# New order, buffer and engine tables for a fused RWKV attention and MLP-mixer kernel

## The chip, the cores and the metric

The kernel runs on one core of a Trainium2 chip. The metric is the time of one execution on the device in microseconds; a run's number is the median of its executions. A profiled execution also has a span, from its first to its last instruction, which is a little shorter than its time.

## The reference

Two stages, float32 in and out. First a linear attention with decay, for batch 4, 8 heads, 768 steps and head size 48:

```python
for t in range(S):
    kt, vt, rt = (k[:, :, t], v[:, :, t], r[:, :, t])
    cur = np.einsum('bhd,bhe->bhde', u[None] * kt, vt)
    y[:, :, t] = np.einsum('bhd,bhde->bhe', rt, state + cur)
    state = w[None, :, :, None] * state + np.einsum('bhd,bhe->bhde', kt, vt)
```

Its output, as x of shape (4, 768, 384), goes through a token mixer and a channel mixer:

```python
h = np.maximum(xt @ w_tok1, 0.0) @ w_tok2      # xt: x with steps and channels turned; d_tok 256
u = x + h.transpose(0, 2, 1)
h2 = np.maximum(u @ w_ch1, 0.0) @ w_ch2        # d_ch 1536
return u + h2
```

## The kernel before, in words

Each batch's 768 steps are six chunks of 128 ("b1 c4" is batch 1, chunk 4). Within a chunk the recurrence is a masked product: k and r are scaled by powers of the decay (tiles `kr`), turned so that the head dimension lies on the partitions (`trk` and `tr_ps` on PE and then `rka` and `rkb` for batches 0 and 1; by a DMA transpose into `rk` for batches 2 and 3), multiplied into scores (`at_ps`), masked on DVE (`AT`), and multiplied with v (`vb`) into `y_ps`. The state goes from chunk to chunk through `kv_ps` and `S`. The term with u is a row sum `adg` times v (`yd` or `ydb`); in batches 2 and 3 the row sum comes from two POOL products, `ku` and `rku`, and a reduction on DVE. The sum is the chunk's part of `x_b`.

When a batch's six chunks are there, the mixer follows: hidden (`h_ps` from `x_b` and `wtok`), relu into `h1r`, back (`hT_ps` or `hx_ps`), the sum u (`u_sb`) and its turned form `uT` (by PE for batch 0 and half of batch 1, by a DMA transpose otherwise). The channel MLP of a batch is two halves of 384 steps: 12 steps `up` a half, each three matmuls into `z_ps` (the "z triple"), a relu into `zr`, and then `down`, in which each of three 128-step tiles takes 12 matmuls in three groups of four into `h_ps`; then `osb` and the store.

Nothing of this runs in the order of the code. The function `add` records each operation as a task with a number (in the order of recording), and `Plan.run` emits the tasks in the order of the table `ORDER`. Each engine works through its own part of that order and never passes one task by another, so an instruction that waits holds all behind it on its engine; DMAs issued by SP are held in the same way in SP's queue, and the weight loads in POOL's. Four tables were written by a planner outside the kernel:

- `ORDER`, the order of all tasks.
- `BUFS`, which buffer of each pool each allocation takes. A new tile in a buffer waits for the readers of the old one. Pool `m` has seven PSUM banks, shared by all results of PE but the state.
- `ENGINES`, for each task recorded by `flex` (relus, copies, casts, products) which of its two engines runs it.
- `W_DEP` and `GATES`: for each of the seven weight loads a load of k, r or v that it waits for, and for some loads a weight load that they wait for. Keys are (batch, chunk, which of k, r, v).

The weight loads are, in order: wtok1, wtok2, the first part of wch1 (columns of the first four up steps), its second part (the other eight), and three parts of wch2. `NWARM` warm-up matmuls on a tile of zeros are tasks of PE, and `FILL` names tasks ahead of which PE gets one more. The engine wrapper records every instruction at one place, so all carry line 281 in the profile, and groups are told apart by their tiles.

In batches 2 and 3 the scaled products run on POOL alone (`POOL_ONLY`).

Of the kernel before, what the change touches and what calls it, by code (L numbers as in the profile page):

```python
# [67 lines left out]
    0, 1, 2, 0, 1, 0, 2, 1, 0, 2, 1, 0, 2, 1, 0, 1, 2, 0, 1, 2, 0, 1, 2, 0,  # L68
],
    'AT1': [  # L70
    0, 1, 2, 0, 1, 0, 2, 1, 0, 2, 1, 0, 2, 0, 1, 2, 0, 1, 2, 0, 1, 2, 0, 1,
# [11 lines left out]
    0, 1, 2, 3, 4, 1, 0, 2, 3, 4, 1, 0, 2, 3, 1, 4, 0, 2, 3, 4, 1, 0, 2, 3,  # L83
# [6 lines left out]
    0, 1, 2, 3, 4, 5, 0, 1, 4, 2, 3, 0, 4, 5, 1, 2, 3, 0, 5, 4, 1, 2, 3, 0, 5, 2, 1, 0, 3, 4,  # L90
# [3 lines left out]
    0, 1, 2, 3, 4, 5, 0, 1, 2, 3, 4, 5, 0, 1, 2, 3, 4, 5, 0, 1, 2, 3, 5, 4,  # L94
],
    'ku': [
    0, 1, 2, 0, 0, 0, 2, 0, 1, 2, 1, 2,
# [13 lines left out]
],  # L111
    'osb': [
    0, 1, 2, 0, 1, 2, 2, 2, 1, 0, 0, 1, 2, 0, 1, 2, 0, 1, 2, 0, 1, 2, 0, 1, 2,
],
    'pr': [
    0, 1, 1, 0, 1, 0, 1, 0, 1, 0, 1, 1,
# [3 lines left out]
    0, 1, 2, 3, 0, 1, 3, 2, 0, 1, 2, 3,  # L120
# [9 lines left out]
    0, 1, 0, 1, 0, 1, 0, 1, 0, 1, 0, 1,  # L130
],
    'rt': [
    0, 1, 2, 3, 4, 0, 1, 2, 4, 0, 3, 1,
# [3 lines left out]
    0, 1, 2, 3, 1, 0, 3, 2,  # L137
# [3 lines left out]
],  # L141
    'vb': [
    0, 1, 2, 3, 4, 0, 1, 3, 2, 4, 0, 1, 2, 3, 0, 3, 4, 1, 3, 1, 2, 0, 4, 3,
],
    'vb2': [],
    'vt': [
    0, 1, 2, 3, 4, 5, 0, 1, 3, 2, 4, 5, 0, 1, 3, 2, 4, 5, 0, 1, 3, 2, 4, 5,
],
    'win': [
    0, 1, 2, 1, 0, 2,  # L150
],
    'yd': [
    0, 1, 2, 0, 1, 2, 0, 1, 2, 0, 1, 0, 2, 1, 0, 1, 2, 0,
],
    'ydb': [
    0, 1, 0, 1, 0, 1,
],
    'zr': [
    0, 1, 2, 1, 0, 1, 2, 0,
],  # L160
}
ENGINES = [
# [12 lines left out]
NWARM = 12  # L175
WIDE_AT = [
    0, 1, 2, 3, 4, 5, 6, 7, 8, 9, 10, 11,
]
FILL = {159: 1}
POOL_ONLY = [  # L180
    2, 3,
]
# [1027 lines left out]
```

## Time and profile before

| | |
|---|---|
| median of 3 runs | 164.02 us (163.69 to 164.03) |
| profiled execution | 163.92 us, span 162.2 us, mean granted clock 0.989 |
| PE busy | 153.4 us, 95% of the span |
| DVE, ACT, POOL busy | 112.1, 68.7, 88.8 us |
| DMA | 26.89 MB, 166 GB/s; 87794 of 93061 packets under 512 B |
| chain that ended last | PE 75%, DMA 11%, POOL 5%, DVE 4% |

The chain of waits is followed back from the last instruction; a share of 75% for PE says that for most of the span the next thing to happen was PE's next matmul. Busy times are sums over the span: matmuls overlap each other in the record, so PE's busy time is not its work at full rate. POOL's products take about 1.0 us each (1000 ns for `kr`, 999 for `ku`), the same product on DVE 0.55.

### The profile page before, as it was taken

Reading aid. Unit: us, or ns where it says so; the run is one execution under the profiler, and the core shown is the slowest. Engines: PE = TensorE matmul, PEld = TensorE weight load, DVE = VectorE, ACT = ScalarE, POOL = GpSimd, SP = SyncE. Lnnn points to the kernel's source line nnn. Section 1 sums busy time; section 2 is a strip of 40 time slices with the busy share of each in tenths; the row PEclk is TensorE's granted clock in tenths of the full one; section 3 lists DMA queues with packets and bytes.
Section 4 is the critical chain, followed back from the end, with each engine's and each line's share of the span. In section 5 each row is a group of like instructions: output and inputs, shape, how many; then the busy total and the mean of one; then the engine's idle time right before and its main releaser. Section 6 shows DMA issues by size and latency. Waiting matters only on the chain.

```text
span 162.2 us, 3788 instructions
## 1 busy us (share of the span) xinstructions
PE 153.4 (95%) x1458; PEld 102.5 (63%) x1459; DVE 112.1 (69%) x237; ACT 68.7 (42%) x150; POOL 88.8 (55%) x112
## 2 busy tenths in 40 slices
PE   6887989599999999999999999999999999999992
PEld 1355667367777667676667766676576666666662
DVE  6599994675697569297969928887998257523432
ACT  3988974437942354255434431144214101355000
POOL 7149891009088899799992987999922000000000
PEclk9996899999999999999999999999999999999999
DMA  5999999999999969999999899998792055300222
GB/s 130 221 206 186 161 246 236 208 178 205 200 180 204 174 137 180 230 211 141 240 213 211 177 192 163 220 207 213 121 251 103 0 124 191 73 6 0 96 98 97
DMA packets 93061, 26.89 MB, mean 166 GB/s; under 512 B 87794, under 2 KB 92148, under 8 KB 93044
## 3 DMA queue, kind: packets, MB, share of 16 engines
q1 hardware_dynamic: 90688, 23.40, 73.7%
q0 software_dynamic: 2160, 3.15, 11.5%
q8 instruction: 11, 0.18, 0.5%
q10 hardware_dynamic: 196, 0.11, 0.2%
q14 instruction: 6, 0.05, 0.1%
HBM read 20.46 MB, written 4.72 MB: 155 GB/s over the span
## 4 chain that ended last, share of the span: by engine, by line
PE 75%; DMA 11%; POOL 5%; DVE 4%; issue 2%; ACT 1%; SPq 1%; POOLq 0%; DVEq 0%
PE h_ps L281 33%; PE z_ps L281 24%; DMA wch<-in_moe_w_ch_dram 5%; PE y_ps L281 4%; PE at_ps L281 3%; DMA win<-in_r_dram 3%; PE hT_ps L281 3%; PE kv_ps L281 2%; DMA kt<-in_k_dram 2%; PE trk L281 2%; POOL kr L281 2%; POOL ydb L281 2%; DVE kr L281 1%; PE hx_ps L281 1%; SPq L281 1%
## 5 line engine op out<-in xcount | busy, mean ns | idle before, releaser
L281 PE MATMUL z_ps<-uT,wch 128*128 128x384 bf16 x288 | 52.5, 327 | 1.8 <-DMA wch<-in_moe_w_ch_dram 1.7
L281 PE MATMUL h_ps<-wch,zr 128*128 128x384 bf16 (+1 forms) x300 | 53.9, 319 | 0.0
L281 ACT ACTIVATE zr<-z_ps 128x384 bf16<-128x384 f32 x56 | 27.1, 491 | 41.0 <-PE z_ps L281 40.7
L281 PEld LDWEIGHTS <-wch 128*128 128x128 bf16 x288 | 31.1, 114 | 14.6 <-DMA wch<-in_moe_w_ch_dram 2.2
L281 PEld LDWEIGHTS <-zr 128*128 128x128 bf16 x300 | 27.6, 98 | 15.4 <-issue 0.2
L281 DVE TENSOR_TENSOR AT<-at_ps,mask 128x512 bf16<-128x512 f32 x48 | 30.9, 684 | 3.0 <-PE at_ps L281 3.0
L281 DVE TENSOR_SCALAR zr<-z_ps 128x384 bf16<-128x384 f32 x40 | 21.3, 554 | 11.9 <-PE z_ps L281 9.2
L281 POOL TENSOR_TENSOR yd<-vb,adg 128x384 f32<-128x384 bf16 x18 | 14.8, 829 | 13.0 <-DVE adg L281 5.2
L281 POOL TENSOR_TENSOR kr<-kt,wnat 128x384 bf16<-128x384 f32 x19 | 19.3, 1018 | 2.7 <-DMA kt<-in_k_dram 2.5
L281 ACT CAST vb<-vt 128x384 bf16<-128x384 f32 x22 | 11.1, 513 | 11.5 <-DMA vt<-in_v_dram 9.7
L281 PEld LDWEIGHTS <-kr 128*128 128x128 bf16 x176 | 11.4, 100 | 6.6 <-POOL kr L281 2.0
L281 DVE TENSOR_TENSOR osb<-u_sb,h_ps 128x384 f32<-128x384 bf16 (+1 forms) x16 | 8.4, 528 | 9.9 <-PE h_ps L281 9.4
L281 POOL TENSOR_TENSOR ku<-kt,u_bc 128x384 f32<-128x384 f32 x12 | 12.1, 1009 | 0.8 <-DMA kt<-in_k_dram 0.8
L281 POOL TENSOR_TENSOR rku<-ku,rt 128x384 f32<-128x384 f32 x12 | 11.9, 1004 | 0.4 <-DMA rt<-in_r_dram 0.3
L281 POOL TENSOR_TENSOR kr<-rt,wp 128x384 bf16<-128x384 f32 x12 | 12.0, 1000 | 0.0
L281 PEld LDWEIGHTS <-wtok 128*128 128x128 bf16 x78 | 7.4, 98 | 4.5
L281 DVE TENSOR_TENSOR x_b<-y_ps,yd 128x384 bf16<-128x384 f32 x18 | 9.6, 552 | 0.5 <-PE y_ps L281 0.5
L281 PE MATMUL y_ps<-vb,AT 128*128 128x48 bf16 x192 | 9.0, 184 | 0.0
L281 POOL TENSOR_TENSOR pr<-rka,rkb 128x512 bf16<-128x512 bf16 x2 | 2.3, 1152 | 11.9 <-DVE rka L281 11.9
L281 PE MATMUL h_ps<-x_b,wtok 128*128 128x384 bf16 x48 | 8.8, 326 | 0.0
L281 ACT CAST S<-kv_ps 48x192 bf16<-48x192 f32 x18 | 5.6, 311 | 6.4 <-PE kv_ps L281 3.3
L281 DVE TENSOR_TENSOR u_sb<-x_b,hT_ps 128x384 bf16<-128x384 bf16 x15 | 7.6, 548 | 0.6 <-PE hT_ps L281 0.6
(92 smaller groups left out, 183.1 us busy)
## 6 DMA issues: line engine op xcount, KB each, us to landing
kt<-in_k_dram SPq DMA_DIRECT2D x24, 192.0 KB, 5.1
vt<-in_v_dram SPq DMA_DIRECT2D x24, 192.0 KB, 4.7
out_dram<-osb SPq DMA_DIRECT2D x23, 192.0 KB, 1.9
win<-in_r_dram SPq DMA_DIRECT2D x6, 384.0 KB, 5.1
rt<-in_r_dram SPq DMA_DIRECT2D x12, 192.0 KB, 3.4
wch<-in_moe_w_ch_dram POOLq DMA_DIRECT2D x4, 384.0 KB, 6.8
wtok<-in_moe_w_tok_dram POOLq DMA_DIRECT2D x2, 384.0 KB, 5.9
wch<-in_moe_w_ch_dram POOLq DMA_DIRECT2D x1, 768.0 KB, 12.2
```

The lines of the kernel that those rows point to most:

```text
L281: return lambda *args, **kw: tc.keep_in_program_order(f(*args, **kw))
```

## The change

`ORDER`, `BUFS` and `ENGINES` are replaced as a whole; `W_DEP` and `GATES` are new; two warm-up matmuls and the one fill are gone; an unused empty list is added. No function and no task but those three matmuls changes. 105 tasks change their engine. The planner that wrote the new tables priced a load at 1.07 times its length if the load ahead of it is of the same tensor and 0.92 times otherwise, and judged an order by its mean over six courses of the execution.

```diff
 ORDER = [
-    0, 3, 22, 54, 18, 6, 16, 8, 895, 42, 59, 21, 896, 43, 39, 23, 53, 7, 13, 24, 19, 9, 2, 14, 56, 1, 11,
...
+    0, 3, 13, 54, 18, 6, 8, 895, 1, 19, 56, 2, 14, 896, 4, 42, 15, 17, 5, 59, 9, 7, 24, 43, 11, 22, 39, 53,
...
 ]
 BUFS = {
     'AT0': [
-    0, 1, 2, 0, 1, 0, 2, 1, 0, 2, 1, 0, 2, 1, 0, 1, 2, 0, 1, 2, 0, 1, 2, 0,
+    0, 1, 2, 1, 0, 2, 1, 0, 2, 1, 0, 2, 1, 0, 2, 1, 0, 2, 1, 2, 0, 1, 2, 0,
...
 ENGINES = [
-    0, 0, 1, 0, 1, 1, 1, 1, 1, 0, 1, 0, 1, 1, 1, 0, 0, 0, 1, 0, 1, 1, 1, 1, 0, 1, 1, 0, 0, 0, 1, 1, 0, 0, 0,
...
+    0, 1, 1, 0, 0, 1, 1, 1, 1, 1, 1, 0, 0, 1, 1, 0, 0, 0, 1, 0, 0, 1, 1, 0, 0, 1, 1, 0, 0, 0, 0, 1, 1, 0, 0,
...
 ]
-W_DEP = [(0, 2, 2), (0, 5, 0), (0, 5, 0), (0, 3, 2), (1, 2, 2), (1, 1, 2), (1, 5, 0)]
-GATES = {(2, 0, 2): 1, (2, 4, 1): 3, (3, 1, 0): 2, (3, 1, 1): 6, (3, 5, 2): 5}
-NWARM = 12
+W_DEP = [(0, 2, 2), (0, 4, 2), (0, 3, 0), (0, 1, 2), (1, 2, 2), (1, 3, 0), (1, 2, 0)]
+GATES = {(2, 0, 1): 4, (2, 3, 1): 2}
+NWARM = 10
 WIDE_AT = [
-    0, 1, 2, 3, 4, 5, 6, 7, 8, 9, 10, 11,
+    0, 1, 2, 3, 4, 5, 6, 7, 8, 9,
 ]
-FILL = {159: 1}
+FILL = {}
+TOKQ = []
```

What moves, where the prediction speaks of it (orders of the two programs, engine by engine):

| | before | after |
|---|---|---|
| SP, loads of batch 0 (rw: r window of two chunks) | rw0, rw2, k0, k1, rw4, v1, k3, k2, k4, v0, v2, v3, v4, k5, v5 | rw0, k1, rw2, k0, rw4, k2, k4, v0, v1, k3, v4, v2, k5, v3, v5 |
| POOL, from wGm to wch1 | wGm x2, wtok1, ydb c0, ydb c2, kr c5, wtok2, ydb c3, ydb c4, wch1 both parts | wGm x2, kr c3, ydb c1, wtok1, ydb c0, ydb c2, pr c3, wtok2, ydb c4, ydb c3, wch1 first part, ydb c5, wch1 second part |
| POOL, end of batch 2 | yd c2, c3, c5, c4 | yd c1, c5, c2, c3, c4 |
| POOL, last products of batch 3 | those of c4 and c5 in turn | those of c3, then of c4: kr, ku, kr, rku |
| SP, ahead of k of b3 c4 | a transpose into uT, k of c4 | uT, two rk, uT, a store, r of c4, k of c4 |
| DVE, the sum adg of b3 c4 | after adg c3 and the sum x of c0 | after x of c0 and an output sum, ahead of two relus and all masks of c2 and c3 |

More of the change, by code (lines that the diff above doesn't have):

```diff
@@ L67 @@
     'AT0': [
-    0, 1, 2, 0, 1, 0, 2, 1, 0, 2, 1, 0, 2, 1, 0, 1, 2, 0, 1, 2, 0, 1, 2, 0,
+    0, 1, 2, 1, 0, 2, 1, 0, 2, 1, 0, 2, 1, 0, 2, 1, 0, 2, 1, 2, 0, 1, 2, 0,
 ],
     'AT1': [
-    0, 1, 2, 0, 1, 0, 2, 1, 0, 2, 1, 0, 2, 0, 1, 2, 0, 1, 2, 0, 1, 2, 0, 1,
+    0, 1, 2, 0, 1, 2, 0, 1, 2, 0, 1, 2, 0, 2, 1, 0, 2, 1, 0, 2, 1, 0, 2, 0,
 ],
@@ L82 @@
     'adg': [
-    0, 1, 2, 3, 4, 1, 0, 2, 3, 4, 1, 0, 2, 3, 1, 4, 0, 2, 3, 4, 1, 0, 2, 3,
+    0, 1, 2, 3, 4, 0, 1, 2, 3, 4, 0, 1, 2, 3, 4, 0, 1, 2, 3, 0, 1, 4, 2, 3,
 ],
@@ L89 @@
     'kp': [
-    0, 1, 2, 3, 4, 5, 0, 1, 4, 2, 3, 0, 4, 5, 1, 2, 3, 0, 5, 4, 1, 2, 3, 0, 5, 2, 1, 0, 3, 4,
+    0, 1, 2, 3, 4, 5, 1, 2, 4, 3, 0, 5, 4, 2, 1, 3, 5, 0, 4, 2, 1, 5, 3, 0, 4, 1, 3, 0, 5, 2,
 ],
@@ L93 @@
     'kt': [
-    0, 1, 2, 3, 4, 5, 0, 1, 2, 3, 4, 5, 0, 1, 2, 3, 4, 5, 0, 1, 2, 3, 5, 4,
+    0, 1, 2, 3, 4, 5, 0, 1, 2, 3, 4, 5, 0, 1, 2, 3, 4, 5, 0, 1, 3, 2, 4, 5,
 ],
     'ku': [
-    0, 1, 2, 0, 0, 0, 2, 0, 1, 2, 1, 2,
+    0, 1, 2, 0, 0, 2, 1, 2, 0, 1, 0, 1,
 ],
@@ L102 @@
     'm': [
[8 rows of a table removed]
[8 rows of a table added]
 ],
     'osb': [
-    0, 1, 2, 0, 1, 2, 2, 2, 1, 0, 0, 1, 2, 0, 1, 2, 0, 1, 2, 0, 1, 2, 0, 1, 2,
+    0, 1, 2, 2, 0, 0, 0, 2, 1, 2, 1, 2, 1, 0, 2, 1, 0, 2, 1, 0, 2, 1, 0, 2, 1,
 ],
     'pr': [
-    0, 1, 1, 0, 1, 0, 1, 0, 1, 0, 1, 1,
+    0, 1, 0, 1, 0, 1, 0, 1, 0, 0, 1, 0,
 ],
@@ L119 @@
     'rk': [
-    0, 1, 2, 3, 0, 1, 3, 2, 0, 1, 2, 3,
+    0, 1, 2, 3, 0, 1, 3, 2, 0, 1, 3, 2,
 ],
@@ L129 @@
     'rku': [
-    0, 1, 0, 1, 0, 1, 0, 1, 0, 1, 0, 1,
+    0, 1, 0, 1, 0, 0, 0, 1, 0, 1, 0, 1,
 ],
     'rt': [
-    0, 1, 2, 3, 4, 0, 1, 2, 4, 0, 3, 1,
+    0, 1, 2, 3, 4, 0, 2, 1, 3, 0, 4, 0,
 ],
@@ L136 @@
     'uT': [
-    0, 1, 2, 3, 1, 0, 3, 2,
+    0, 1, 2, 3, 0, 1, 3, 2,
 ],
@@ L142 @@
     'vb': [
-    0, 1, 2, 3, 4, 0, 1, 3, 2, 4, 0, 1, 2, 3, 0, 3, 4, 1, 3, 1, 2, 0, 4, 3,
+    0, 1, 2, 3, 4, 1, 0, 2, 4, 3, 1, 0, 2, 4, 3, 4, 1, 4, 3, 2, 4, 0, 1, 2,
 ],
@@ L146 @@
     'vt': [
-    0, 1, 2, 3, 4, 5, 0, 1, 3, 2, 4, 5, 0, 1, 3, 2, 4, 5, 0, 1, 3, 2, 4, 5,
+    0, 1, 2, 3, 4, 5, 0, 1, 3, 4, 2, 5, 0, 1, 3, 4, 2, 5, 0, 1, 3, 4, 2, 5,
 ],
     'win': [
-    0, 1, 2, 1, 0, 2,
+    0, 1, 2, 0, 1, 2,
 ],
     'yd': [
-    0, 1, 2, 0, 1, 2, 0, 1, 2, 0, 1, 0, 2, 1, 0, 1, 2, 0,
+    0, 1, 2, 0, 2, 1, 0, 2, 1, 0, 2, 0, 2, 1, 0, 2, 1, 0,
 ],
@@ L158 @@
     'zr': [
-    0, 1, 2, 1, 0, 1, 2, 0,
+    0, 1, 2, 1, 0, 2, 1, 0,
 ],
```

116 rows, old and new, of tables (BUFS, ENGINES, ORDER) are left out of this document.

## The prediction

> **What bounds the kernel now.** I read the page first, then the chain of waits in order of time, then each engine's timeline around the two places where that chain leaves PE. From the page:
>
> ```profile
> span 162.2 us, 3788 instructions
> PE 153.4 (95%) x1458; PEld 102.5 (63%) x1459; DVE 112.1 (69%) x237; ACT 68.7 (42%) x150; POOL 88.8 (55%) x112
> PE   6887989599999999999999999999999999999992
> DMA  5999999999999969999999899998792055300222
> ```
>
> PE has gaps only in the first eight slices (4.05 us each), and after that none. DMA is as full until about 115 us. The chain and PE's own timeline say what ends the early gaps:
>
> ```profile
> 23.36 8.75 DMA wch<-in_moe_w_ch_dram
> 32.15 3.12 PE L281 MATMUL z_ps<-uT,wch 128*128 128x384 bf16 x18 [1.71 <-DMA wch<-in_moe_w_ch_dram]
> ```
>
> The first line is a piece of the chain (start, length): the first part of wch1, issued by POOL at 23.36 and landed at 32.1. The second is PE's first step of the channel MLP, 1.71 us idle ahead of it. From there to the last matmul (159.26) PE runs 127.1 us.
>
> To see what of that is waiting I add up PE's steps in the program's order at the chain's own prices: z triple 0.487, four down matmuls 0.65, y 0.37, a pair of scores 0.55, kv 0.17, a turn of k 0.22, hidden 1.95, back 0.327. The sum from the first z to the end is 124.6, so 2.5 us are lost. Beside PE's timeline: batch 3's second kv stands at 32.15+67.7 = 99.85 by the sum and at 101.14 in the trace (1.3 lost); batch 3's state product of chunk 3 at 116.05 and 118.37 (2.3 lost); the last back step at 133.35 and 135.82 (2.5). So 1.0 us goes in one place, 101 to 118. There the chain leaves PE:
>
> ```profile
> 104.68 3.44 DMA kt<-in_k_dram
> 108.21 1.00 POOL kr L281
> 110.91 1.02 POOL rku L281
> 111.95 0.55 DVE adg L281
> 113.89 0.94 DVE zr L281 x2
> 114.88 1.14 PE z_ps L281 x6
> ```
>
> A late load of k holds POOL, POOL's rku holds DVE's row sum adg, and adg, in order on DVE, holds the relus zr that empty PE's PSUM buffers. Nothing else in the 127 us is long. What can be won there is at most 2.5 us, what can be lost is open.
>
> **The change part by part.** All four tables that order and place the work are new; the tasks are the same but for two warm-up matmuls and one fill. Since every useful matmul stays, the end is the first z's start, plus 124.6, plus PE's waits.
>
> Warm-ups: two of 128x512 (one at 15.03 took 0.63) and the fill (17.41, 0.32) go. They stood where PE waits for POOL's kr anyway, and nothing is earlier by them: 0.
>
> Load order up to the first z. In the trace the loads of batch 0 land about 1 us apart per 192 KB (r windows count two): the landing is 4.7 for the first window, 9.8 after eight units, 15.1 after thirteen, 20.2 after seventeen. In the new SP order v of chunk 0 is unit 11 instead of 13 (13.0, was 15.1), v of chunk 2 unit 15 instead of 14, k of chunk 3 unit 13 instead of 10. So POOL has: kr of chunks 2 and 4 to 13.2; the two wGm (0.95 each; their scales come from ACT after v of chunk 0's cast, 13.6) to 15.6; kr of chunk 3 to 16.6; ydb of chunk 1, taken over from DVE (0.80), to 17.4; then wtok1 is issued, at 17.4 where it was 17.04. After it come ydb of 0 and 2, the product pr of chunk 3 (1.15, was DVE's), wtok2 at 21.2 (was 21.16), two ydb, and wch1's first part at 23.5 to 23.7 (was 23.36), its second part after one more ydb at 25 (was about 24.1). The four landed at 22.6, 27.4, 32.1 and 36.3, one after the other, so the first's delay passes down: between +0.1 and +0.4; I take **+0.3** for the first z. The x chain beside it (state, masks, y, hidden, back) comes out at 26.4 for the last x where it was 26.68; the 1.71 us hide it, and it costs only beyond that. The second part is first needed after eight z triples, a turn and a score, 4.4 us after the first z, 36.9; by the series it lands at 36.6 to 37.3: 0 to 0.4, taken as 0. [...]
>
> Gates: of five, none delays anything in the trace (the gated loads are issued after 50 us, the weights have landed by 58); the new ones hold r of batch 2 chunk 0 for wch2's first part. It is issued near 42 and lands 5.4 to 7.5 later; POOL uses that r near 60: 0.
>
> Batch 1's attention (z of batch 0 beside it). Eight steps of it move from POOL to DVE and five from DVE to POOL. By the sum, y of chunk 1 stands at 14.5 after the first z (was 17.1), its scores end at 12.7, and three masks of 0.6 (the pitch of AT in DVE's timeline) end at 14.65: +0.15. kv_id of chunk 2, at 16.4, needs S, behind one more mask, yd, rka: 16.7: +0.3 in all. From there DVE holds 5.8 us until kr of chunk 4, which PE turns at 22.2: the 0.3 stays. With a cast as slow as the 0.93 at 53.98 it becomes 1.0; with every wait hidden 0. I take **+0.4**. POOL then waits for that chunk 3 cast before it can start batch 2: 55.6 instead of 54.65.
>
> Batch 2. 24 products of POOL at a pitch of 0.957, seven yd of 0.8 and the 0.75 that it waited for a load of k here before end at 84.9; the last yd waits for a buffer that x of chunk 2 frees (84.6) where it was chunk 3's (88.2). So POOL can start batch 3 at 85, not 89.0.
>
> uT of batch 2. Its transpose by DMA took 4.0 from issue (99.71) to landing, and another 5.1. In the new order PE has 69.4-64.3 = 5.1 us of work between the last back step of that half and the z that needs it (was 6.1), of which 0.65 go to u_sb; SP no longer has a transpose of rk just ahead. 0 to +0.75: **+0.2**.
>
> Batch 3. The old wait goes: the scores of chunks 2 and 3 stand at 81.4 instead of 79.9, their POOL products end near 108: **-1.0**. But chunk 4's loads now come last: k is behind four transposes and a store on SP, issued near 106.3, landed 109.8 to 111.4 (3.5 to 5.1 as the other k loads); POOL does four products, rku last, ending at 113.6 to 115.2. The row sum of chunk 4 stands on DVE ahead of two relus and all masks of chunks 2 and 3, and PE is there at 32.45+79.7+1.5 = 113.65 (1.3 lost as before, 0.2 for uT), with about 1 us of PSUM buffers in hand. That is 0 to +1.2: **+0.5**, the middle.
>
> Tail: z and down end as before, with the two half stores behind the last down: 0, and at most one such half sum of DVE, 0.35, either way.
>
> Sum: 0.3+0.4+0.2-1.0+0.5 = **+0.4**. Against the profiled execution (163.92, its span 162.2 and 1.7 around it) that is a span of 162.6 and 164.3; the median of the runs is 0.1 above that execution: **164.4**.
>
> **The rivals.** Faster (b): the old wait goes and nothing takes its place. For it: POOL's 4 us lead into batch 3, and DVE 69% busy. Against it: DVE's two sums in the same place again. Then +0.1-1.0, and the 0.4 lost between 75 and 92 (0.95 to 1.4 against the sum) may go too: 163.1 to 162.7.
>
> No change to speak of (c): the price of a load may not be what decides. In SP's timeline a load after one of its own tensor takes 1.07 to 1.15, after another 0.90 to 1.0, so the effect is there; the new order has three repeats fewer in batch 0, 0.45 us. But the first z waits for POOL's queue, not for these loads, so the change may do what it says and move nothing: 163.7 to 164.3.
>
> Much slower (d): POOL's lead is lost at the k load of batch 3 chunk 4. If it lands after 112.5 (SP held by a store that waits, as it was from 54 to 58.4), POOL's rku ends after 116.3, DVE's row sum follows, and everything behind it: 2 us beyond the point, 113.65+1, from which it decides: 164.02+0.9-1.0+2.0 = 165.9. For it: the chain shows this very path; against it: no store before it is late by my sum.
>
> Another slow case sits in (d): the clock.
>
> ```profile
> 12.00:14.00 2.00, 1.47 (x28) 0.99 (x25) 1.96 (x7) 1.96 (x8) 1.84 (x2) 0.93 1.39 187
> 14.00:16.00 2.00, 1.57 (x9) 1.02 (x10) 1.82 (x4) 1.39 (x3) 1.94 (x4) 0.50 1.35 187
> 16.00:18.00 2.00, 1.92 (x31) 1.40 (x31) 2.00 (x5) 1.82 (x6) 2.00 (x2) 0.72 1.40 194
> ```
>
> (The last columns are granted clock, DMA, GB/s; PE's busy share is the first.) After a sparse stretch the grant was halved for some 3 us. Fewer warm-ups could bring that on at the first z: 3.4 us at half clock, +1.7. The 1.71 us idle before the first z left it at 1.00 here, so 3 in 100. [...]
>
> **How the numbers follow.** Forecast 0.39 (its own range 163.8 to 165.3), (b) 0.35, (c) 0.13, (d) 0.13. A measurement tells 0.2%, 0.33 us, from no change. Faster: (b) and a little of the forecast's low end, 0.36; same: (c) and the forecast's edge, 0.15; slower 0.49. The range from (b)'s low end, 162.6, to just beyond (d), 166.2, leaves out 2 in 10: unseen waits above, a smoother middle below.
>
> **What would show it.** Right: wtok1 issued at 17.3 to 17.6 and the first z at 32.3 to 32.6, still behind wch; the scores of batch 3 chunks 2 and 3 without a wait; adg of chunk 4 waiting for rku near 114, PE idle behind zr. Wrong: a first z off by over 0.7 either way; PE's waits after it summing to under 1.5 (then b) or over 4 us (then d, or a place that I have not found); a granted clock under 1 after 30 us.

## The result, and the profile after

The changed kernel takes 165.25 us (median of 12; 164.41 to 168.11), the kernel before 163.49 beside it: ratio 1.0124, 95% interval 1.0098 to 1.015. On another chip it was 165.33 against 163.66: ratio 1.006 (1.0025 to 1.0095); the ratios leave out runs more than 1.5% above the fastest of their kernel, five of twelve there, so the medians stand beside them. Slower by 1.0 to 2.0 us, then, where +0.4 was forecast: the sign was right, the size was not.

The profiled execution took 166.15 us, 2.2 us more than that of before, in span too (164.4). From its page:

```profile
PE 154.5 (94%) x1456; PEld 103.0 (63%) x1456; DVE 113.5 (69%) x238; ACT 69.3 (42%) x151; POOL 87.6 (53%) x111
PE   6988999599999999999999979999979999999992
```

PE has two new dips, in slices 24 and 30 (4.1 us each: 94.5 to 98.6 and 119.2 to 123.3). PE's timeline (start, length, then the idle time ahead and what ended it) names them:

```profile
32.40 2.63 PE L282 MATMUL z_ps<-uT,wch 128*128 128x384 bf16 x15 [1.66 <-DMA wch<-in_moe_w_ch_dram]
96.66 0.33 PE L282 MATMUL kv_ps<-vb,kr 128*128 128x96 bf16 x4 [0.90 <-ACT vb L282]
104.36 0.68 PE L282 MATMUL z_ps<-uT,wch 128*128 128x384 bf16 x3 [0.19 <-DMA uT<-u_sb]
120.34 0.33 PE L282 MATMUL kv_ps<-vb,kr 128*128 128x96 bf16 x4 [0.89 <-ACT S L282]
```

The first is the first z, 0.25 later than before (forecast +0.3). The second is kv of batch 3 chunk 0, which waits for ACT's cast of v. In the kernel before it ran without a wait:

```profile
99.67 0.33 PE L281 MATMUL kv_ps<-vb,kr 128*128 128x96 bf16 x4
```

The third waits for the transpose of u, the fourth, kv of chunk 4, for ACT's copy of the state S of chunk 3. In the chain of waits (start, length) both kv steps lead back to a load of v:

```profile
91.68 4.34 DMA vt<-in_v_dram
96.10 0.52 ACT vb L282
114.05 5.10 DMA vt<-in_v_dram
```

and ACT's timeline shows how the second load gets at S: the cast vb of chunk 5, for which ACT waited 3.02 us, stands ahead of S in ACT's order.

```profile
119.23 0.51 ACT L282 CAST vb<-vt 128x384 bf16<-128x384 f32 x1 [3.02 <-DMA vt<-in_v_dram]
119.65 0.65 ACT L282 CAST S<-kv_ps 48x192 bf16<-48x192 f32 x2
```

Against the same sum of PE's steps as in the prediction (124.6 us from the first z), the loss after the first z is 4.5 us where it was 2.5: 1.2 by batch 2's hidden step (1.3 before), 2.3 behind kv of chunk 0, 3.05 at the state product of chunk 3 (2.3 before), 4.05 behind kv of chunk 4. So of the 2.2 us this profile puts 0.25 into the start, -0.1 into batches 1 and 2, and 2.1 into batch 3, where two waits of 0.9 us stand that the prediction does not contain. Waits of over 4 us after the first z were its own sign of "a place that I have not found". The experiments show that this one execution tells half of it.

### The profile page after: what moved, and what is told of

Its sections match the earlier page's. It is cut to its first block, busy times and chain, and to the rows that moved or that the text cites. A ratio compares the mean times of both kernels' runs of the same rounds, so it can differ in the third digit from the quotient of the medians.

```text
span 164.4 us, 3764 instructions
## 1 busy us (share of the span) xinstructions
PE 154.5 (94%) x1456; PEld 103.0 (63%) x1456; DVE 113.5 (69%) x238; ACT 69.3 (42%) x151; POOL 87.6 (53%) x111
## 4 chain that ended last, share of the span: by engine, by line
PE 48%; DMA 16%; POOL 14%; SPq 11%; ACT 5%; issue 3%; DVE 1%; ACTq 0%; POOLq 0%
PE z_ps L282 19%; PE h_ps L282 19%; SPq L282 11%; DMA vt<-in_v_dram 9%; POOL kr L282 5%; DMA wch<-in_moe_w_ch_dram 5%; POOL rku L282 3%; DMA uT<-u_sb 3%; POOL ku L282 3%; PE y_ps L282 2%; PE hT_ps L282 2%; POOL yd L282 2%; ACT vb L282 2%; PE at_ps L282 2%; PE kv_ps L282 2%
## 5 line engine op out<-in xcount | busy, mean ns | idle before, releaser
L282 ACT ACTIVATE zr<-z_ps 128x384 bf16<-128x384 f32 x57 | 27.7, 491 | 41.6 <-PE z_ps L282 41.4
L282 POOL TENSOR_TENSOR yd<-vb,adg 128x384 f32<-128x384 bf16 x15 | 12.7, 848 | 15.3 <-DVE x_b L282 7.1
L282 PEld LDWEIGHTS <-kr 128*128 128x128 bf16 x176 | 12.2, 104 | 7.7 <-issue 3.5
L282 DVE TENSOR_REDUCE adg<-rku 128x8 f32<-128x384 f32 x12 | 6.6, 550 | 4.0 <-POOL rku L282 4.0
L282 POOL TENSOR_TENSOR pr<-rka,rkb 128x512 bf16<-128x512 bf16 x3 | 3.5, 1153 | 10.4 <-DVE rka L282 10.4
L282 ACT CAST S<-kv_ps 48x192 bf16<-48x192 f32 x20 | 6.3, 313 | 6.5 <-PE kv_ps L282 5.1
```

Source lines behind the costliest of these rows:

```text
L282: return lambda *args, **kw: tc.keep_in_program_order(f(*args, **kw))
```

## The experiments

The late-v theory: the two v loads are the cause. Its rival, the whole-stage theory: batch 3's loads and POOL's series set the pace, and a wait removed comes back at the next step. A third, the start theory, came out of the first four runs. In the edits, numbers in ORDER are steps, emitted in that order; ENGINES holds the engine of each movable step.

**e1_v0_early, e2_s3_first, e3_both, e4_kv0_late.** Edits of ORDER: 103 is the load of v of batch 3 chunk 0, 111 that of r of chunk 3; 765 is the copy of S of chunk 3, 777 the cast of v of chunk 5; 729 is kv of chunk 0, 730 its state's copy, 735 kv of chunk 1.

```diff
 e1:
-    104, 516, 612, 710, 586, 611, 111, ..., 317, 610, 505, 718, 103,
+    104, 516, 612, 710, 586, 611, 103, ..., 111, 317, 610, 505, 718,
 e2:
-    755, 661, 782, 764, 763, 777, 650, 765,
+    755, 661, 782, 764, 763, 765, 777, 650,
 e3: both
 e4: 729, 730 to right ahead of step 500, 735 behind step 501
```

> The changed kernel with two loads of batch 3 exchanged in SP's order: v of chunk 0 where r of chunk 3 was (issued near 87.8 instead of 91.7), r of chunk 3 after it. Late-v theory: PE's kv of batch 3 chunk 0 (0.90 us idle before it, at 96.66) has its cast vb at about 92.7 and waits no more; the uT transpose, u_sb and all behind come 0.9 to 1.0 earlier; the second wait (kv of chunk 4, 0.89) stays: 164.3 where the changed kernel had 165.25. Whole-stage theory (batch 3's loads as a series at 1 us each and POOL's products behind them set the pace, and kv is only where it shows): POOL's k and r products are as late as before, the 0.9 comes back at the next step that waits for POOL (scores of chunks 0 and 1, 110.5): within 0.2 us of 165.25. Start theory (the time is lost ahead of batch 3): no change, 165.25.

> The changed kernel with one step moved on ACT: the copy of the state S of batch 3 chunk 3 ahead of the cast vb of chunk 5, which waits for a v load that lands at 119.2. In-order-ACT theory: S is copied at about 117.9 to 118.6 instead of 119.65 to 120.3, PE's kv of chunk 4 (0.89 idle before it, at 120.34) does not wait: 0.8 to 0.9 earlier, 164.4. Whole-stage theory: the scores of chunks 4 and 5, at 122.5, wait for the transposes of POOL's last products (issued at 115.3, done at 119.3), and y of chunk 5 for the late vb; the wait moves there, gain under 0.3: 165.0 to 165.25.

> The changed kernel with both edits: v of chunk 0 exchanged with r of chunk 3 in SP's order, and the copy of S of chunk 3 ahead of vb of chunk 5 on ACT. Late-v theory: the two waits are independent, 165.25 less 0.95 and less 0.85: 163.4 to 163.6, equal to the kernel before (163.49). Whole-stage theory: gain under 0.5 in all, 164.8 to 165.25. If a single one of the two counts: 164.3.

> The changed kernel with no load moved, but PE's kv of batch 3 chunk 0 (and the copy of its state on ACT) put 3.0 us of PE work later, behind the last two back steps of batch 2 and one z triple; kv of chunk 1 follows two down steps behind it. Late-v theory in its PE form (the load comes when it came in the kernel before, 91.7 and 91.4; only the step that reads it was moved ahead): PE passes 96.7 with back steps that are ready, kv runs near 99 with no wait: 0.8 to 1.0 less, 164.3, as with the earlier load. Whole-stage theory: within 0.2 of 165.25. If the state's copy between kv of chunks 0 and 1 costs PE, 0.2 to 0.3 of the gain is given back: 164.6.

Measured: 165.0, 164.82, 165.28 and 164.93 us, ratios 1.0055 (1.0019 to 1.0091), 1.007 (1.0037 to 1.0103), 1.0066 (1.0025 to 1.0107), 1.0079 (1.0045 to 1.0113). Each wait goes where it was taken away (with both edits no kv waits; in e1's profile the second is gone too, though nothing was moved there), but one edit brings about as much as both, and both far from all. With kv of chunk 0 put later (e4) PE waits 1.16 us at the next back step instead: its PSUM buffer is emptied by ACT (osb at 96.91), behind the same cast (vb at 96.49, which waited 1.81 us for its load). And something else shows. The first 80 us of these kernels are those of the changed kernel, yet the first z came at 34.12, 33.17, 33.29 and 32.61, each time without a wait for wch. In e4, from the timelines of DVE, POOL and PE:

```profile
19.43 2.10 DVE L283 TENSOR_TENSOR kr<-kt,wnat 128x384 bf16<-128x384 f32 x1 [1.54 <-DMA kt<-in_k_dram]
18.37 1.64 POOL L283 TENSOR_TENSOR ydb<-vb,adg 128x384 bf16<-128x384 bf16 x2
19.95 1.16 POOL L283 TENSOR_TENSOR pr<-rka,rkb 128x512 bf16<-128x512 bf16 x1
21.92 0.58 PE L283 MATMUL trk<-ident,kr 128*128 128x128 bf16 x4 [1.99 <-DVE pr L283]
32.61 2.60 PE L283 MATMUL z_ps<-uT,wch 128*128 128x384 bf16 x15
```

and in the changed kernel's own profile:

```profile
18.28 0.63 DVE L282 TENSOR_TENSOR kr<-kt,wnat 128x384 bf16<-128x384 f32 x1 [0.20 <-DMA kt<-in_k_dram]
17.55 1.03 POOL L282 DMA_DIRECT2D wtok<-in_moe_w_tok_dram  x1 [0.44 <-DMA vt<-in_v_dram]
18.59 1.79 POOL L282 TENSOR_TENSOR ydb<-vb,adg 128x384 bf16<-128x384 bf16 x2
```

In the kernel before, POOL made this product kr of batch 0 chunk 5, in 1.00 us:

```profile
20.22 1.00 POOL L281 TENSOR_TENSOR kr<-kt,wnat 128x384 bf16<-128x384 f32 x1 [0.52 <-DMA kt<-in_k_dram]
```

On DVE it took 0.63 us in the changed kernel's profile, where it started while POOL only issued a load (17.55 to 18.58), and 2.10 in e4, where its k landed 1.2 us later, beside POOL's ydb, ydb and pr. It ends at 21.53, 0.42 after pr (21.11). A late k is not needed for it: in e3 kr began at 18.44, without a wait for its load, as POOL's first ydb began (18.48), and took 3.20. PE's turn of kr then waits 1.99; what ended that wait by the record is DVE's next product pr, which stands right behind kr. So the x chain (state, masks, y and x of batch 0), not wch, sets the first z in these four profiles. The product pr of chunk 3 on POOL, 1.15 us of that series, is new too. Granted clock (third column from the right, ahead of DMA share and GB/s) in e4 and in the changed kernel, from 16 us on:

```profile
16.00:20.00 4.00, 3.71 (x55) 2.64 (x52) 2.31 (x6) 3.95 (x9) 3.56 (x6) 0.70 1.28 163
20.00:24.00 4.00, 2.08 (x26) 1.62 (x27) 3.78 (x7) 2.41 (x6) 2.02 (x4) 0.72 1.23 225
```

```profile
16.00:20.00 4.00, 3.55 (x48) 2.63 (x44) 2.97 (x8) 3.80 (x8) 3.55 (x5) 0.57 1.24 160
20.00:24.00 4.00, 3.68 (x70) 2.76 (x70) 3.55 (x8) 3.69 (x11) 3.46 (x5) 1.00 1.19 206
```

By this column the grant is halved once in the changed kernel's profile, from 16.5 to 19.9. In e4 (0.87 from 12 to 16 and 0.85 from 24 to 28) it is halved twice, from 15.0 to 18.4 and, from the end of the stretch in which PE waited, from 21.7 to 25.1: 3.4 us each. In e1 (0.85, three times 0.50, 0.94 from 12 to 32) it stays halved from 14.8 to 28.4.

**f1_pr3_dve, f2_before_swap, f3_warm, f4_all3.** These try the start: pr back on DVE, the same exchange put into the kernel before, the missing warm-ups put back, and all three edits together. (The warm-ups of f3 write over the first state product of batch 0.)

```diff
 f1 (changed kernel), engine of pr of batch 0 chunk 3:
-ENGINES[39] = 0   # POOL
+ENGINES[39] = 1   # DVE
 f2 (kernel before): ENGINES[39] 1 -> 0, ENGINES[54] (kr of chunk 5) 0 -> 1
 f3 (changed kernel):
-NWARM = 10        # FILL = {}
+NWARM = 12        # FILL = {159: 1}
-    147, 141, 155,
+    147, 141, 905, 906, 155,
 f4: e3 and f1
```

> The changed kernel with one step of batch 0 given back: the product pr of chunk 3 on DVE, as in the kernel before, instead of POOL (1.15 us there, at 20.3). In four runs of kernels whose first 80 us are those of the changed kernel, DVE's product kr of chunk 5 (both inputs in SBUF) took 2.1 to 3.2 us instead of 0.63, and ended each time (21.5 to 21.8) with POOL's series of two ydb and this pr; scores, x and the first z (32.6 to 34.1 instead of 32.4, and no longer behind wch1) followed. Port theory: without pr in the series DVE's kr ends by 20.5; the first z is behind wch1 again, and that is issued up to 1 us earlier since POOL is free earlier: first z 31.5 to 32.6 in the profile, median 0.6 to 1.0 below the changed kernel's 165.25, 164.3 to 164.6. Clock theory (the first z is late because the granted clock was halved for two to four windows of 3.4 us from 14 us on): kr's length is a symptom; the clock is still 0.96 to 0.98, median within 0.3 of 165.25. Late-v theory alone: the start costs 0.25 and no more, so within 0.2.

> The kernel before with the same exchange of engines put into it: kr of batch 0 chunk 5 on DVE instead of POOL, pr of chunk 3 on POOL instead of DVE, places in the order kept. Port theory: kr on DVE (0.55 alone) stands behind POOL's series and takes 2 to 3 us where POOL works beside it, the scores of chunk 5 and the first z come later by 0.5 to 1.5: 164.0 to 164.8 against 163.5. Clock theory: no warm-up is touched, 163.5, and the clock stays at 0.979 to 0.99. Late-v theory: 163.5.

> The changed kernel with the two warm-ups of 128x512 and the fill of 128x384 put back on PE between the first kv of batch 0 and the turn of k of chunk 4 (about 14.5 us) and at y of chunk 1. Clock theory: the halved windows go back to one or two, clock 0.979 to 0.99 in all runs, the first z near 32.4, median 164.4 to 164.8. Port theory: the clock may rise, kr of chunk 5 still takes 2 to 3 us, and the first z is still 32.6 to 34: median within 0.3 of 165.25. Late-v theory: within 0.2 of 165.25.

> The changed kernel with three edits: v of batch 3 chunk 0 exchanged with r of chunk 3 on SP, the copy of S of chunk 3 ahead of vb of chunk 5 on ACT, and pr of batch 0 chunk 3 on DVE. Two-lane theory: a late first z and the late v loads hide each other, so that each edit alone gives 0.3 to 0.9 and only all three give the whole: 163.0 to 163.5, as the kernel before (163.5) or up to 0.5 better. Additive theory: 165.25 less 0.75 (start), less 0.6 (both others, as measured together): 163.9. If the start does not matter: 164.6 as with the other two edits alone.

Measured: f1 164.16, ratio 1.0032 (1.0001 to 1.0063); f2 164.06, 1.0025 (0.9989 to 1.006); f3 165.84, 1.0136 (1.0093 to 1.0179); f4 163.79, 1.0015 (0.9979 to 1.0051); the kernel before 163.83. In f1, with kr late again (19.40):

```profile
19.40 1.09 DVE L283 TENSOR_TENSOR kr<-kt,wnat 128x384 bf16<-128x384 f32 x1 [1.44 <-DMA kt<-in_k_dram]
20.00 0.61 POOL L283 DMA_DIRECT2D wtok<-in_moe_w_tok_dram  x1
32.16 2.63 PE L283 MATMUL z_ps<-uT,wch 128*128 128x384 bf16 x15 [0.81 <-DMA wch<-in_moe_w_ch_dram]
```

kr ends at 20.49, 0.42 after the last ydb, and the first z waits for wch again. The part of the expectation that wch1 would be issued earlier failed: 24.15, as in the changed kernel, since POOL then waits 1.98 us for DVE. In f2 kr took 1.62 us and the first z came at 32.65 without a wait, but the time can't be told from no change. f3 answers the clock: it was 0.979 to 1.00 in its six runs, and the time no better. In its profile kr started in time (0.62 us); what its other runs paid at the start is not shown. That profile has the earliest first z of all, and the same waits in batch 3:

```profile
30.95 2.63 PE L283 MATMUL z_ps<-uT,wch 128*128 128x384 bf16 x15 [0.22 <-DMA wch<-in_moe_w_ch_dram]
96.16 0.33 PE L283 MATMUL kv_ps<-vb,kr 128*128 128x96 bf16 x4 [0.80 <-ACT vb L283]
```

A first z 1.45 us earlier moves kv of batch 3 chunk 0 by 0.5 (96.66): it waits for the load of v, which runs beside PE and sets that time. So the two causes partly hide each other, as f4's expectation had it.

**g1_pr_later, g2_before_k2, g3_all3_warm, g4_v0_late.** 186 is pr of chunk 3, 120 the issue of wtok2; 107 is the load of k of batch 3 chunk 2, 716 the transpose of rk of chunk 0.

```diff
 g1 (changed kernel): 186 from ahead of 120 to right behind it
 g2 (kernel before):  107 to right ahead of 716
 g3: f4, NWARM = 12, FILL = {159: 1}, and
-    168, 147, 141,
+    168, 905, 906, 147, 141,
 g4: f1, and 103 to right behind 106 (v of chunk 1); the buffers of v in BUFS follow
```

> The changed kernel with no step on another engine: only the product pr of batch 0 chunk 3 stands on POOL behind the issue of wtok2 instead of ahead of it, so that POOL's series beside DVE's kr of chunk 5 is two ydb (1.6 us) instead of two ydb and pr (2.7). Port theory (kr, both inputs in SBUF, ends only when POOL's series ends): kr ends by 20.5 as with pr on DVE, the first z near 32.2 behind wch1, 164.0 to 164.5 (pr on DVE gave 164.16). POOL-load theory (pr's 1.15 us on POOL is the cost wherever it stands): wch1's issue is as late as in the changed kernel, 165.0 to 165.5.

> The kernel before with one load moved: k of batch 3 chunk 2, issued at 97.17 behind a transpose (94.36, waiting for POOL) and a store, goes ahead of both, to about 94.4. POOL waited 1.16 us for it at 101.54, and by the prediction's chain (POOL rku, DVE's row sum adg, the relus, PE's PSUM buffers) that is the 1.0 us that PE loses between 101 and 118. Prediction's theory: 0.7 to 1.0 less, 162.6 to 163.0 against 163.6. Rival: POOL's 1.16 us only move to the next load of its series (r of chunk 3, k of chunk 5, each 1 us apart): within 0.3 of 163.6.

> The changed kernel with the three edits (v of batch 3 chunk 0 earlier, copy of S of chunk 3 ahead of vb of chunk 5, pr of batch 0 chunk 3 on DVE; 163.79 together) and with the two warm-ups and the fill back, ahead of the first kv of batch 0. Two-lane theory: the clock stays at 0.99 to 1.0 and the first z comes at 31 to 32, but loads and POOL's series set the times of batch 3 as before, so at most half of it reaches the end: 163.3 to 163.8. Clock theory: all of it reaches the end, 162.6 to 163.2.

> The changed kernel with pr of batch 0 chunk 3 on DVE (164.16) and the suspected wait made longer: v of batch 3 chunk 0 goes three loads later on SP, behind v of chunk 4, r and v of chunk 1 (issued near 94 instead of 91.1). Late-v theory: PE's kv of chunk 0 waits until about 98.5 instead of 95.5, 2 to 3 us, the last back steps, u_sb and uT behind it, and the end is later by 1.5 to 3: 165.7 to 167. Whole-stage theory (batch 3's pace is set by POOL's series): under 0.7 of it reaches the end: 164.2 to 164.9.

g1: 166.35, ratio 1.0119 (1.0051 to 1.0187), where the port theory (kr ends only when POOL's series ends) expected 164.0 to 164.5. That is above its rival's 165.0 to 165.5 too. In the profiled run (167.14, the longest of six) kr was held here as well:

```profile
19.50 2.75 DVE L283 TENSOR_TENSOR kr<-kt,wnat 128x384 bf16<-128x384 f32 x1 [1.55 <-DMA kt<-in_k_dram]
20.04 0.60 POOL L283 DMA_DIRECT2D wtok<-in_moe_w_tok_dram  x1
20.66 1.17 POOL L283 TENSOR_TENSOR pr<-rka,rkb 128x512 bf16<-128x512 bf16 x1
35.05 1.14 PE L283 MATMUL z_ps<-uT,wch 128*128 128x384 bf16 x6
```

POOL has no tensor product from 20.11 to 20.66, and kr doesn't end there, as it did in f1: it ends at 22.25, again 0.42 after pr. Why it did not end in that gap is not shown. PE's z begins at 35.05, 2.65 later than in the changed kernel's profile, but the span is only 1.0 longer (165.4): the waits behind the late start were shorter.

g4: 168.82, ratio 1.0246 (1.0172 to 1.032), 4.7 us over f1, more than expected. The v load was issued at 93.84 instead of 91.11:

```profile
98.63 0.48 PE L284 MATMUL kv_ps<-vb,kr 128*128 128x96 bf16 x4 [3.12 <-ACT vb L284]
100.00:104.00 4.00, 4.00 (x16) 2.01 (x15) 2.14 (x5) 0.89 (x2) 3.30 (x4) 0.50 0.00 0
```

PE waits 3.12 us, all of it new, and the clock is halved from 97.6, still in the wait, to 104.4 (the second line: PE busy all 4 us, clock 0.50; it is 0.70 from 96 to 100 and 0.95 from 104 to 108). From kv's start on that is 5.8 us at a clock of 0.50. Six matmuls into hT_ps take 1.92 us there in the chain, where six took 0.97 in the kernel before; at this rate, by estimate, 2.9 us of PE's work are lost: the clock costs about as much as the wait. (The profiled runs of g4 and f1 lie 5.9 us apart, 169.14 and 163.27.) So the way from that load to the end is real, and the whole-stage theory is wrong on this point.

g3: 164.5, ratio 1.004 (0.9997 to 1.0082): the clock at 0.978 to 1.00 adds nothing that can be told to f4 (1.0015 on another chip). g2: 163.56, ratio 0.9986 (0.9949 to 1.0023), not told apart from the kernel before, so the prediction's price of 1.0 for the old wait isn't confirmed; 0.7 to 1.0 less was expected, and the rival's 0.3 fits. Where POOL waits in it instead is not shown.

**h1_v0_ahead, h2_v05_ahead, h3_v05_pool.** 594 is the transpose of rk of batch 2 chunk 4, 118 the load of v of chunk 5, 745 the transpose of rk of chunk 2.

```diff
 h1: f1, and 103 to right ahead of 594
 h2: h1, and 118 to right ahead of 745
 h3: h2 with pr on POOL (ENGINES[39] = 0)
```

> The changed kernel with pr of batch 0 chunk 3 on DVE, and v of batch 3 chunk 0 ahead of the transpose of rk of batch 2 chunk 4, at which SP waits from 81 to 83 for POOL: issued near 81 instead of 91.1, the loads behind it no later, or 1 us earlier from its old place on. Late-v theory: kv of chunk 0 never waits, in runs too where its load lands late; ratio to the kernel before 1.000 to 1.002, after 1.003 without it. Rival (kv had no wait left once the start was repaired, and the loads behind the old place are what counts): within 0.1% of 1.003.

> As the one above, and v of batch 3 chunk 5 ahead of the transposes of rk of chunks 2 and 3 (issued near 108.5 instead of 112 to 114). Late-v theory: the cast vb of chunk 5 no longer holds the copy of S on ACT, 0.1 to 0.5% less: ratio 0.997 to 1.000, 163.2 to 163.7. Rival: the two transposes come 0.5 later and the scores of chunks 2 and 3 with them: no gain, 1.001 to 1.003.

> The changed kernel with both v loads ahead as above, but pr of batch 0 chunk 3 left on POOL. Port theory: DVE's kr of chunk 5 takes 2 to 3 us again in most runs and the first z comes at 32.6 to 34; ratio 1.005 to 1.008, 0.5 to 0.8% above the same with pr on DVE. Late-v theory as the whole cause: 0.999 to 1.002.

Measured: 165.0, 165.27 and 165.69 against 164.11; ratios 1.0063 (1.003 to 1.0097), 1.0063 (1.0034 to 1.0093), 1.0077 (1.0041 to 1.0113). h1 and h2 came out above what either theory expected, and no better than pr on DVE alone (f1, 1.0032). No kv waits in any of the three profiles, and PE waits further on; in h2:

```profile
103.60 0.68 PE L284 MATMUL z_ps<-uT,wch 128*128 128x384 bf16 x3 [0.98 <-DMA uT<-u_sb]
111.01 2.11 PE L284 MATMUL z_ps<-uT,wch 128*128 128x384 bf16 x12 [0.55 <-DVE zr L284]
```

What the late v loads held back is held next by the transpose of u and by DVE's relus, the two waits that the prediction did name. So lengthening the v wait costs all of it and more (g4), taking it away gives little or nothing: the whole-stage theory is right that far.

**k1_after_again, k2_pr3_dve, k3_all3** are the changed kernel, f1 and f4 on one chip, beside the kernel before (163.66).

> The changed kernel itself, beside the two below on one chip. Its ratio to the kernel before is 1.010 to 1.015 if the first measurement holds on this chip, and in about 1 run of 3 the mean granted clock is 0.97 or less (4 of 12 before).

> The changed kernel with pr of batch 0 chunk 3 on DVE. Start theory (DVE's kr behind POOL's series, then scores, x, the first z, with the clock halved longer): no run with a clock of 0.97 or less, 0.5 to 0.9% less than the changed kernel beside it: ratio 1.003 to 1.007. Late-v theory as the main cause: 0.1 to 0.3% less: 1.009 to 1.012.

> The changed kernel with pr on DVE, v of batch 3 chunk 0 earlier, and the copy of S ahead of vb of chunk 5. Start theory: 0.1 to 0.3% less than with pr alone, since uT and the relus are next behind the two waits: 1.001 to 1.005. Late-v theory: 0.5% or more less than with pr alone.

| | median us | ratio (95%) | runs with a clock of 0.97 or less |
|---|---|---|---|
| changed kernel | 165.33 | 1.006 (1.0025 to 1.0095) | 4 of 12 |
| pr on DVE | 164.51 | 1.0034 (1.0005 to 1.0063) | 0 of 12 |
| all three edits | 164.08 | 1.0031 (1.0001 to 1.0062) | 0 of 12 |

By the medians the start costs 0.8 us, the two v waits 0.4 more, and 0.4 stays. By the ratios the first is 0.26% (0.4 us), with intervals that overlap, and the second nothing; the start's price on this chip is thus between 0.4 and 0.8, the v waits' between 0 and 0.4. Across chips it would be more: 1.0124 for the changed kernel in the first measurement, 1.0032 with pr on DVE (f1). With pr on DVE a wait of the v kind can still come: in k2's profile kv of chunk 4 waited 1.23 us for S.

```profile
119.59 0.33 PE L283 MATMUL kv_ps<-vb,kr 128*128 128x96 bf16 x4 [1.23 <-ACT S L283]
```

The clock tells the two starts apart better than the times: over all kernels with pr ahead on POOL or beside the issue of wtok2, and no added warm-up (the changed kernel twice, e1 to e4, g1, h3), 32 of 90 runs had a mean clock of 0.97 or less; with pr on DVE (f1, f4, h1, h2, k2, k3) 0 of 72. The pair h3 and h2, with this one engine between them, has 6 of 12 and 0 of 12. f2, the same exchange in the order and with the warm-ups of the kernel before, has 1 of 12. No version tried beats the kernel before by more than can be told.

## Why the prediction was right or wrong

- **The first z, +0.3: right in the profile** (32.15 to 32.40, behind wch, with wtok1 issued at 17.55 for 17.4). **Wrong as a rule: this is the step that failed first.** The prediction let the x chain end at 26.4 and the 1.71 us hide it. It did in both profiles of the changed kernel (PE 1.66 and 1.35 us idle ahead of z for wch, last x at 27.0 in the first), but not in e1 to e4 and g1, where the first z came at 32.6 to 35.05 with no wait. The term left out is one step, kr of chunk 5 from POOL to DVE: the prediction priced only what the exchange did to POOL's queue, and took DVE's product at its length alone. In five profiles (e1 to e4, g1) it took 2.1 to 3.2 us beside POOL's series with pr in it, instead of 0.63. The runs put this in place of the hidden x chain, at 0.4 to 0.8 us of the time (k1 against k2). That kr is late in some runs of the changed kernel itself is inferred, from its clock (8 of 24 runs at 0.97 or less) and from kernels with the same first 80 us: neither of its two profiles shows it.
- **kr beside POOL's products.** kr ended 0.42 us after the series of two ydb and pr in e1 to e4, 0.42 after the two ydb in f1, and 0.42 after pr in g1, there across 0.55 us without a tensor instruction on POOL (20.11 to 20.66). What holds it is not shown; the name port theory stands for this observation alone. DVE's pr, whose input trk lies in PSUM, took 0.42 us in the midst of POOL's pair of ydb (18.59 to 20.38) in the changed kernel's profile, and 0.41 at 22.21, while POOL ran no tensor instruction:

```profile
19.28 0.42 DVE L282 TENSOR_TENSOR pr<-trk,rkb 128x512 bf16<-128x512 bf16 x1 [0.37 <-ACT rkb L282]
```

- **Warm-ups at 0: right, as far as runs on different chips tell.** With them back the clock was 0.978 or more in all 18 runs (f3, g3), and no time was gained. The clock case of rival (d), 3 in 100, named a halved clock at the first z; in e4 and g1 it was halved again ahead of it, behind the wait for kr (1.99 and 2.34 us; in e4 from 21.7, and in g1 six matmuls into h_ps at 27.53 took 2.10 us, where e4's took 1.14). By this order it is there more a mark of the late start than its cause.
- **Batch 1, +0.4: mis-sized.** The loss is 0.75 at batch 1's hidden step (PE at 63.65 for 62.9 by the sum) and was 0.76 before (64.41 for 63.65): 0.
- **uT of batch 2, +0.2: right** in the profile (0.19 idle); without the v wait ahead of it it grew to 0.6 to 1.0 (0.83, 0.69, 0.98 and 0.62 in e1, e3, h2 and k3).
- **Batch 3, -1.0 and +0.5: not confirmed, and incomplete.** From kv of chunk 1 to the state product of chunk 3 the loss grew by 0.85 (1.0 before), and g2 shows that the late k load gave little when moved. adg of chunk 4 came at 115.12 (named near 114), but no wait of PE for zr shows behind it. POOL's lead of 4 us into this batch did not last: it began at 87.30 (85 in the prediction, 89.01 before), waited 0.75, 0.94 and 0.97 for loads, and at 95.5 it had started seven products in either program. One of these waits, from POOL's timeline:

```profile
95.03 0.99 POOL L282 TENSOR_TENSOR ku<-kt,u_bc 128x384 f32<-128x384 f32 x1 [0.97 <-DMA kt<-in_k_dram]
```

  Left out was v: the prediction followed the loads of k and r to POOL, not v to ACT and kv. PE's kv of chunk 0 stands at 62.0 in the new sum (66.3 before), and its load is issued at 91.68 as before (91.36): a step moved 4.3 us ahead past a load that stayed. And the copy of S stands behind a cast that waits for a load. Each showed 0.9 us in the profile; the median gives 0.4 for both, since the next waits take most of it.
- **The sum.** What k3 leaves in place, the prediction's own terms, measured +0.42 against the forecast +0.4. That agreement is luck: batch 1's +0.4 measured 0, and neither of batch 3's two terms is confirmed. The rest, 1.25 of 1.67 us by the medians, went with the three edits for the start and the two v waits. Rival (d), 165.9, had the size, but not the place: POOL's lead was lost to the first loads of batch 3, not at the k load of chunk 4.

What stays open: how the 0.4 to 0.8 us of the start divide between the late x chain and the halved clock seen behind it (e4, g1), since in the profiles of both edits with the warm-ups back (f3, g3: clock 0.978 and above) the first z moved too (30.95 and 31.93, where it stood at 32.40 and 31.74 in the changed kernel's and at 32.16 in f4's); and why the ratio of the changed kernel was 1.0124 on one chip and 1.006 on another.

## What to carry to other kernels

When a step changes engine, price it beside what the neighbour engine does at that time, not at its length alone: here DVE's product kr ended 0.42 us after the last product of POOL's series in e1 to e4, f1 and g1, and took 1.09 to 3.20 us where it took 0.63 in the changed kernel's profile. When a planner moves a step of an in-order engine ahead, look up every load behind its inputs, v as well as k and r, and every instruction queued ahead of its producers. One profile of a kernel with two chains of work that are both close to setting the time shows one of them; look at the clock and the first waits of several executions before dividing up a difference of 1%.

## What the runs showed of the hardware that was not expected

- DVE's kr of 128x384 (f32 inputs in SBUF) took 0.60 to 0.72 us where it began at 18.01 to 18.29 (eight profiles); in the changed kernel's two, f3 and f4 that was 0.28 to 0.31 ahead of POOL's first ydb. It took 2.08, 2.10, 2.23 and 3.20 beside ydb, ydb and pr (e2, e4, e1, e3), and 1.09 beside the two ydb alone (f1), each time ending 0.42 us after the last of them. In k3 and h2, where pr is on DVE as in f1, it began at 19.46 and 19.54 and took 1.08 and 1.13. In g1 (2.75) it was held across 0.55 us in which POOL only issued a load. In f2 (1.62) it ended 1.0 after two ydb and 0.43 into the next, which took 1.11 instead of 0.83.
- In h3 kr began at 19.29, 0.77 into POOL's pair of ydb (18.52), and took 0.56; there the pair took 2.01 instead of 1.64. Which product goes first in such a stretch is not settled by these runs.
- A wait of 3.12 us of a busy PE (g4): the granted clock was 0.50 from 97.6, in the wait, to 104.4. In the changed kernel's profile the waits of 1.66, 0.90 and 0.89 us left it at 1.00 (from 30 to 34, 94 to 104 and 118 to 124).
- The same load with nearly the same issue time (k of batch 0 chunk 5, at 13.50 in e4 and 13.62 in the changed kernel) had landed when kr started at 19.43 and 18.28: 1.2 us between two profiles, of which one had its first z at 32.61 without a wait and the other at 32.40 behind wch.
